# The sum's products of a fused attention and feed-forward kernel come in any order of quads, planned far behind h

## Chip, cores and metric

The kernel runs on one core of a Trainium2 chip. The metric is the device time of one execution in microseconds (us); lower is better. The core's engines are TensorE (PE in the profile; its weight loads are PEld), ScalarE (ACT), VectorE (DVE), GpSimd (POOL) and SyncE (SP), which here only issues DMA transfers. Each engine works through its own instructions in the order of the program.

## What is computed

The input x has 4 batches of 12480 rows with 128 channels. Two attention steps are followed by a feed-forward layer (FFN) over all 49920 rows:

```python
def mab(q, kv):
    s = scale * (q @ kv.transpose(0, 2, 1))
    s = s - s.max(-1, keepdims=True)
    a = np.exp(s)
    a /= a.sum(-1, keepdims=True) + 1e-09
    return a @ kv
h = mab(I, x)                       # 32 inducing rows attend to all x of a batch
attn = mab(x, h)                    # every row attends to the 32 rows of h
...
h = np.maximum(x @ w_in, 0.0)       # x is attn here; w_in is 128 x 2048
return (h * h @ w_out)              # w_out is 2048 x 128
```

All is in fp32. The second attention's weighted sum is not made by itself: since attn is a matrix of weights times the batch's 32 rows, the kernel multiplies those rows by w_in once for each batch (hw in the code) and uses the 32 weights of a row as the FFN's input.

## The kernel before

Rows are taken in **units** of 960, 13 for each batch, 52 in all. For each unit three streams of work are woven together:

- the **first attention** of a unit of the next batch (class First): scores of the 32 inducing rows (sp or na on TensorE, line 430), a running maximum (mx, neg), exponentials (e on ScalarE), transposes (ep, et), a matmul with x (hp or nb, line 484) and the running sums hacc and zs;
- the **second attention** of the unit that comes next (class Second): scores (na, line 626), their eviction ss, transposes (s2t), a softmax in small steps (mx, d, z, rz, d, sk), transposes back (ap, line 687), an eviction sw, and four DMAs on SP that spread sw into st;
- the **FFN** of the present unit (ffn_block), in two blocks of 480 rows. A block goes over the 2048 hidden channels in four **quads** of 512.

Scores of the second attention of unit u+1, of the first attention and its matmul with x are issued together by the function narrow, 32 matmuls, which the text calls a group of small matmuls.

A quad j of a block goes like this. TensorE makes h in two pairs of matmuls, each pair into one of two PSUM buffers (line 782). ScalarE takes the relu of each pair into g (line 790) and then squares the whole of g, 1920 columns, in place (line 801). For fp32 accuracy g is split into hi (rounded to the fp32r type) and lo = g - hi. For even quads VectorE makes hi (line 808); for odd ones a casting DMA of the POOL queue does (line 806, "CAST" in the planner). VectorE makes lo of every quad (line 812). TensorE then makes 12 products (line 825) that add to the block's output sum op in PSUM: four with hi and the high part of w_out (wo_hi), four with hi and its low part (wo_lo), four with lo and wo_hi. After the last quad VectorE transposes op into rows (line 840), and SP stores them.

Buffers: g has four, hi three, lo two, h two, op two.

The order on every engine is set by a **planner** (class Plan) when the program is built. Each step is added as a task with an engine, a cost in ns, a due time, the tasks that it needs and the buffers that it takes or reads. The planner then runs the tasks in an imitated time: of the tasks of an engine that can start within 40 ns of when the engine is free, it takes the one with the earliest due time; otherwise the one that can start first. The costs in its lines (438 for a pair of products, 864 for a relu, 1706 for a square, 2070 for lo) are the author's numbers. Block due times advance by PERIOD / 2 = 16000 ns, quads by part = 4000 ns.

Two rules matter here. First, the six tasks of two products each that make up a quad's 12 are chained: each needs the one before it (last), through all four quads of a block, so the sum goes strictly from quad 0 to quad 3 and through hi with wo_hi, hi with wo_lo and lo in that order. Their due time is the quad's plus 8000 ns, that of the pairs of h two quads later. Secondly, narrow for unit u+1 needs begun, the first matmul of h of unit u.

Of the kernel before, what the change touches and what calls it, by code (L numbers as in the profile page):

```python
# [44 lines left out]
class Plan:  # L45
# [15 lines left out]
    def add(self, engine, ns, fn, due, needs=(), port=False, mode=None, takes=(), reads=(), late=None):  # L61

        if late is None:
            late = self.LATE["PE" if engine == "PE" else "other"] if due > self.begin else 0.0
        needs = [n for n in needs if n is not None]
        t = Task(engine.split("|"), ns, fn, due, needs, port, mode, takes, late, len(self.tasks))  # L70
        for b in list(takes) + list(reads):
            b.users.append(t)
        self.tasks.append(t)
        return t
# [80 lines left out]
def induced_attention_then_squared_relu_ffn(  # L155
# [12 lines left out]
    NF = F // P  # L168
# [4 lines left out]
    NQ = NF // 4  # L173
# [5 lines left out]
    LATE_G1, LATE_OT = 150.0, 400.0  # L179
# [51 lines left out]
    add = plan.add  # L231
# [494 lines left out]
    def narrow(second, f, g, due, step, begun=None):  # L726

        v = {}
        bank_a = Buffer("m") if second or f else None
        bank_b = Buffer("m") if g else None  # L730
        needs = [begun]
        if second:
            needs += [second.s["joined"]]
        if f:
            needs += f.turned
        if g:
            needs += [g.et_done]

        def go():
            if bank_a:  # L740
                v["a"] = bank(f"na_{second.n if second else f.n}")
            if second:
                second.score(v["a"][:, :2 * TS])
            if f:
                f.score(v["a"][:, 2 * TS:4 * TS])
            if g:
                v["b"] = bank(f"nb_{g.n}")
                g.mix(v["b"][:, :C])

        t = add("PE", 510 * bool(second) + 520 * bool(f) + 450 * bool(g), go, due, needs, mode="n",  # L750
                takes=[b for b in (bank_a, bank_b) if b],
                reads=([second.bt] if second else []) + ([f.bt] if f else []) + ([g.bx] if g else []))
        if f:
            f.weigh(t, lambda: v["a"][:, 2 * TS:4 * TS], bank_a, due)
        if second:
            second.weigh(t, lambda: v["a"][:, :2 * TS], bank_a, due, step)
        if g:
            g.add_up(t, lambda: v["b"][:, :C], bank_b, due)


    def ffn_block(b, u, k, second, t0, first_needs):
# [2 lines left out]
        w = {}  # L764
        bo = Buffer("o")
        part = PERIOD / 2 / NQ
        last = None

        def quad(j, last):
            v = {}  # L770
            due = t0 + j * part
            bg, bhi, blo = Buffer("g"), Buffer("hi"), Buffer("lo")
# [44 lines left out]
            for m, (wo, name, from_, buf) in enumerate((  # L817
                (wo_hi, "hi", th, bhi), (wo_lo, "hi", th, bhi), (wo_hi, "lo", tl, blo),
            )):
                for i in range(2):  # L820
                    def products(i=i, wo=wo, name=name, m=m):
                        if j == m == i == 0:
                            w["op"] = ps_o.tile([P, 512], F32, tag="o", name=f"op_{n}")
                        for l in (2 * i, 2 * i + 1):
                            nc.tensor.matmul(  # L825
                                w["op"][:, :BLK], wo[:, 4 * j + l, :], v[name][:, l, :],
                                start=(j == m == l == 0), stop=(j == NQ - 1 and m == 2 and l == 3),
                            )

                    begin = j == m == i == 0  # L830
                    last = add("PE", 438, products, due + 8000 + 600 * (2 * m + i), [from_, last, w_outs[j]],
                               takes=[bo] if begin else [], reads=[buf] + ([] if begin else [bo]))
            return last

        for j in range(NQ):
            last = quad(j, last)

        def rows():
            w["rows"] = att.tile([P, BLK // M, M], F32, tag="rows", name=f"rows_{n}")
# [5 lines left out]

        br = Buffer("rows")
        end = t0 + PERIOD / 2 + 8000
        t = add("DVE", 570, rows, end + 1500, [last], reads=[bo], late=LATE_OT, takes=[br])
        add("SP", 2000, store, end + 4000, [t], reads=[br])
        return w["begun"]  # L850

# [18 lines left out]
    for w, (b, u) in enumerate(units):  # L870
        t_u = t_main + w * PERIOD
        begun = [ffn_block(b, u, k, seconds[w], t_u + k * PERIOD / 2, [opened] if w == 0 else []) for k in range(2)][0]
        nxt = units[w + 1] if w + 1 < len(units) else None
        a = w + NU + 1
        f = g = None
        if a < len(units):
            f = firsts[a] = First(*units[a], t_u + NARROW)
        if a - 1 < len(units):
            g = firsts[a - 1]
        if nxt is None:  # L880
            break
        seconds[w + 1] = Second(*nxt) if nxt[1] else None
        if nxt[1] == 0:
            mix_alone(g, t_u - 2000)
            first_end(nxt[0], t_u, 2000)
            seconds[w + 1] = Second(*nxt)
            narrow(seconds[w + 1], f, None, t_u + NARROW, 1700, begun)
        else:
            narrow(seconds[w + 1], f, g, t_u + NARROW, STEP, begun)
    for t in plan.run():  # L890
        t.fn()

# [30 lines left out]
```

## Time and profile before

| what | us |
|---|---|
| time, median of 3 runs (1910.66 to 1913.94) | 1913.87 |
| the profiled execution's own time | 1910.1 |
| its span, from the first instruction to the last | 1908.3 |
| first and last matmul of h, start | 77.7, 1890.9 |
| mean granted clock of TensorE (1 is full) | 0.986 |

The page gives for each engine its busy time, its share of the span and its number of instructions. A group row gives line, engine, operation, what is written and read, the count, then the busy time in us and the mean of one instruction in ns, then the idle time of the engine ahead of them and what ended most of it. A row of waits reads: engine, tile and line, what it waited for, us in total, times, longest. A timeline row reads: start, length, engine, line, operation, names, count, and in brackets the idle time ahead of it with what ended it. "SPq" is the time in which SP issues a DMA. The end of a matmul is modelled, and a matmul's length includes its way through the array, so that the start of the next one is often earlier than the end shown.

### The profile page before, as it was taken

To read this page: it belongs to the slowest core of one execution; us is meant where nothing else is said; L and a number is where in the kernel's file an instruction comes from. 1 tells how busy PE (TensorE), PEld (TensorE's weight loads), DVE (VectorE), ACT (ScalarE), POOL (GpSimd) and SP (SyncE) were. 2 spreads that over 40 slices of the span, in tenths; PEclk is the share of its full clock that TensorE was granted. 3 is DMA by queue.
4 is the path that set the end of the run, shared out by engine and by line. 5 is a ranking of instruction groups with operands and counts; after the bars stand their busy time and mean duration, and the time that the engine had idled before them with its cause. 6 is when DMAs were issued, how large, how long until landed. Compare 5 with 4: busy or idle time off the path is not lost.

```text
span 1908.3 us, 24030 instructions
## 1 busy us (share of the span) xinstructions
PE 1710.5 (90%) x8897; PEld 1342.1 (70%) x8897; DVE 1462.8 (77%) x1548; ACT 1590.1 (83%) x1602; POOL 128.9 (7%) x230
## 2 busy tenths in 40 slices
PE   7698989889998998989998989899999999998997
PEld 4377767777777777777777767777777777776776
DVE  6677777777887777878787778777777877777776
ACT  5578888788888888888888888888888888888886
POOL 1200000000000000000000000000000000000000
PEclk9799999999999999999999999999999999999999
DMA  9656756666666757667747657667444544444453
GB/s 216 121 156 159 179 159 164 174 159 165 168 165 165 177 163 179 162 173 167 190 141 171 157 170 184 163 164 178 145 140 130 161 148 153 134 152 147 141 159 120
DMA packets 458736, 306.12 MB, mean 160 GB/s; under 512 B 366172, under 2 KB 431484, under 8 KB 458620
## 3 DMA queue, kind: packets, MB, share of 16 engines
q1 hardware_dynamic: 428668, 100.11, 30.7%
q0 software_dynamic: 29952, 204.49, 29.6%
q8 instruction: 70, 1.15, 0.3%
q14 instruction: 46, 0.38, 0.1%
HBM read 48.94 MB, written 25.56 MB: 39 GB/s over the span
## 4 chain that ended last, share of the span: by engine, by line
PE 37%; ACT 21%; issue 15%; DVE 14%; DMA 11%; SPq 2%; DVEq 0%; ACTq 0%; POOLq 0%; POOL 0%
PE op L825 27%; ACT g L790 12%; DVE lo L812 7%; ACT g L801 7%; PE h L782 7%; DMA hi<-g 6%; DVE hi L808 3%; DMA xq<-in_x_dram 3%; SPq L397 1%; DMA words_i<-in_moe_w_in_dram 1%; DVE xt L401 1%; PE wp L586 1%; PE na L626 1%; DVE d L655 1%; ACT d L658 1%
## 5 line engine op out<-in xcount | busy, mean ns | idle before, releaser
L790 ACT ACTIVATE g<-h 128x960 f32<-128x960 f32 x832 | 769.5, 970 | 178.1 <-PE h L782 171.3
L812 DVE TENSOR_TENSOR lo<-g,hi 128x1920 fp32r<-128x1920 f32 x416 | 882.4, 2153 | 36.9 <-DMA hi<-g 28.8
L801 ACT ACTIVATE g<-g 128x1920 f32<-128x1920 f32 x416 | 752.7, 1809 | 5.7
L782 PE MATMUL h<-st,hw 128*128 128x480 f32 x1664 | 481.7, 393 | 104.3 <-ACT g L790 100.0
L825 PE MATMUL op<-hi,wo_hi 128*128 128x480 f32 x1664 | 452.4, 392 | 27.4 <-DMA hi<-g 25.3
L825 PE MATMUL op<-lo,wo_hi 128*128 128x480 f32 x1664 | 429.5, 385 | 17.9 <-DVE lo L812 17.5
L782 PEld LDWEIGHTS h<-st,hw 128*128 128x128 f32 x1664 | 298.4, 189 | 201.1 <-ACT g L790 159.0
L825 PE MATMUL op<-hi,wo_lo 128*128 128x480 f32 x1664 | 429.6, 383 | 0.0
L808 DVE CAST hi<-g 128x1920 fp32r<-128x1920 f32 x208 | 240.8, 1158 | 227.5 <-ACT g L801 226.1
L825 PEld LDWEIGHTS op<-hi,wo_hi 128*128 128x128 f32 x1664 | 303.6, 190 | 103.4 <-DMA hi<-g 41.7
L825 PEld LDWEIGHTS op<-lo,wo_hi 128*128 128x128 f32 x1664 | 305.7, 188 | 81.9 <-DVE lo L812 37.3
L825 PEld LDWEIGHTS op<-hi,wo_lo 128*128 128x128 f32 x1664 | 315.9, 190 | 51.6 <-issue 1.4
L806 POOL DMA_DIRECT2D hi<-g x208 | 110.6, 532 | 1701.6 <-ACT g L801 1366.3
L840 DVE STREAM_TRANSPOSE rows<-op 128x480 f32<-128x480 f32 x104 | 70.7, 679 | 82.6 <-PE op L825 82.6
L658 ACT ACTIVATE d<-d 120x256 f32<-120x256 f32 x52 | 21.7, 417 | 55.4 <-DVE d L655 55.4
L687 PEld LDWEIGHTS ap<-identr,sk 120*128 120x128 f32 x208 | 28.3, 190 | 37.5 <-DVE sk L680 30.6
L687 PE MATMUL ap<-identr,sk 120*128 120x120 f32 x208 | 32.6, 279 | 21.5 <-DVE sk L680 21.2
L401 DVE STREAM_TRANSPOSE xt<-xq 128x960 f32<-128x960 f32 x39 | 45.8, 1174 | 3.9 <-PE na L626 3.8
L651 DVE TENSOR_REDUCE mx<-s2t 120x8 f32<-120x256 f32 x52 | 21.8, 419 | 20.2 <-PE s2t L644 20.0
L662 DVE TENSOR_REDUCE z<-d 120x8 f32<-120x256 f32 x52 | 20.8, 401 | 17.0 <-ACT d L658 17.0
L235 ACT COPY et<-ep 120x256 f32<-120x256 f32 x52 | 19.4, 374 | 16.7 <-PE ep L464 16.0
L626 PE MATMUL na<-xt,hT 128*32 128x240 f32 x416 | 32.7, 387 | 0.0
(91 smaller groups left out, 611.1 us busy)
## 6 DMA issues: line engine op xcount, KB each, us to landing
hi<-g POOLq DMA_DIRECT2D x208, 960.0 KB, 4.1
xn<-in_x_dram SPq DMA_DIRECT2D x52, 480.0 KB, 5.2
st<-sw SPq DMA_DIRECT2D x208, 120.0 KB, 2.3
out_dram<-rows SPq DMA_DIRECT2D x416, 60.0 KB, 2.0
xq<-in_x_dram SPq DMA_DIRECT2D x156, 120.0 KB, 4.4
words_i<-in_moe_w_in_dram SPq DMA_DIRECT2D x4, 512.0 KB, 9.2
words_o<-in_moe_w_out_dram SPq DMA_DIRECT2D x4, 512.0 KB, 7.5
ind_sb<-in_inducing_dram SPq DMA_DIRECT2D x1, 16.0 KB, 1.7
```

Source lines behind the costliest of these rows:

```text
L401: nc.vector.transpose(self.xt, v["xq"].rearrange("p g c -> p (g c)"))
L626: nc.tensor.matmul(where[q * M:(q + 1) * M, :].rearrange("m (k t) -> m k t", k=2), self.s["hT"][:, :M], self.s["xt"][self.u].rearrange("c ...
L658: nc.scalar.activation(v["d"], v["d"], AF.Exp, scale=scale)
L687: nc.tensor.matmul(ap[:, q * TS:(q + 1) * TS], v["sk"][:, q].rearrange("t k a m -> t (k a m)"), identr[:TS, :TS], start=(q == 0), stop=(q ...
L782: nc.tensor.matmul(c["hp"][:, l, :BLK], s["hw"][:, f * P:(f + 1) * P], s["st", u][:, k, :], start=True, stop=True,)
L790: nc.scalar.activation(v["g"][:, 2 * i:2 * i + 2, :], c["hp"][:, :, :BLK], AF.Relu)
L801: nc.scalar.activation(v["g"], v["g"], AF.Square)
L806: nc.gpsimd.dma_start(v["hi"], v["g"])
L808: nc.vector.tensor_copy(v["hi"], v["g"])
L812: nc.vector.tensor_sub(v["lo"], v["g"], v["hi"])
L825: nc.tensor.matmul(w["op"][:, :BLK], wo[:, 4 * j + l, :], v[name][:, l, :], start=(j == m == l == 0), stop=(j == NQ - 1 and m == 2 and l = ...
L840: nc.vector.transpose(w["rows"].rearrange("p g c -> p (g c)"), w["op"][:, :BLK])
```

## The change

The six product tasks of a quad no longer need each other. They need only the first product task of the block, which opens the sum (it takes the PSUM buffer op); which matmul starts and which ends the accumulation is now counted while the program is written out (done). Their due time is the quad's plus 18000 ns in place of 8000. The transpose of op needs all of the block's 24 product tasks (sums) in place of the last. And narrow is called without begun, so it needs only what it reads. The number and shape of TensorE's instructions are unchanged, as are all costs in the planner. Lines behind line 767 have other numbers: h is line 783, the products are 827, lo is 813.

```diff
-        last = None
-
-        def quad(j, last):
+        sums, done = [], []
+
+        def quad(j):
...
-                    def products(i=i, wo=wo, name=name, m=m):
-                        if j == m == i == 0:
+                    def products(i=i, wo=wo, name=name):
+                        if not done:
                             w["op"] = ps_o.tile([P, 512], F32, tag="o", name=f"op_{n}")
                         for l in (2 * i, 2 * i + 1):
+                            done.append(l)
                             nc.tensor.matmul(
                                 w["op"][:, :BLK], wo[:, 4 * j + l, :], v[name][:, l, :],
-                                start=(j == m == l == 0), stop=(j == NQ - 1 and m == 2 and l == 3),
+                                start=len(done) == 1, stop=len(done) == 3 * NF,
                             )
 
-                    begin = j == m == i == 0
-                    last = add("PE", 438, products, due + 8000 + 600 * (2 * m + i), [from_, last, w_outs[j]],
-                               takes=[bo] if begin else [], reads=[buf] + ([] if begin else [bo]))
-            return last
+                    begin = not sums
+                    sums.append(add(
+                        "PE", 438, products, due + 18000 + 600 * (2 * m + i), [from_, w_outs[j]] + sums[:1],
+                        takes=[bo] if begin else [], reads=[buf] + ([] if begin else [bo]),
+                    ))
...
-        t = add("DVE", 570, rows, end + 1500, [last], reads=[bo], late=LATE_OT, takes=[br])
+        t = add("DVE", 570, rows, end + 1500, sums, reads=[bo], late=LATE_OT, takes=[br])
...
-            narrow(seconds[w + 1], f, None, t_u + NARROW, 1700, begun)
+            narrow(seconds[w + 1], f, None, t_u + NARROW, 1700)
         else:
-            narrow(seconds[w + 1], f, g, t_u + NARROW, STEP, begun)
+            narrow(seconds[w + 1], f, g, t_u + NARROW, STEP)
```

What this does to the order is shown at three places. In the names, h_2_6_1_4 is the fifth pair of h (from 0) of batch 2, unit 6, block 1; hi_2_6_0_3 is hi of quad 3 of block 0; the last number of a name only numbers the buffers.

On TensorE, in block 1 of unit 6 of batch 2, before:

```order
L782 MATMUL h_2_6_1_4_10761<-st_2_6_10417,hw_2_8476 128x480 x2
L825 MATMUL op_2_6_1_10766<-hi_2_6_1_0_10758,wo_hi_110 128x480 x4
L825 MATMUL op_2_6_0_10635<-hi_2_6_0_3_10734,wo_hi_110 128x480 x4
L825 MATMUL op_2_6_0_10635<-hi_2_6_0_3_10734,wo_lo_111 128x480 x4
L825 MATMUL op_2_6_1_10766<-hi_2_6_1_0_10758,wo_lo_111 128x480 x4
L782 MATMUL h_2_6_1_5_10790<-st_2_6_10417,hw_2_8476 128x480 x2
L825 MATMUL op_2_6_1_10766<-lo_2_6_1_0_10764,wo_hi_110 128x480 x2
L825 MATMUL op_2_6_0_10635<-lo_2_6_0_3_10780,wo_hi_110 128x480 x4
L825 MATMUL op_2_6_1_10766<-lo_2_6_1_0_10764,wo_hi_110 128x480 x2
L782 MATMUL h_2_6_1_6_10803<-st_2_6_10417,hw_2_8476 128x480 x2
L782 MATMUL h_2_6_1_7_10808<-st_2_6_10417,hw_2_8476 128x480 x2
L782 MATMUL h_2_7_0_0_10820<-st_2_7_10715,hw_2_8476 128x480 x2
```

The same place after the change:

```order
L783 MATMUL h_2_6_1_4_10755<-st_2_6_10447,hw_2_8485 128x480 x2
L827 MATMUL op_2_6_0_10657<-hi_2_6_0_2_10668,wo_lo_111 128x480 x2
L827 MATMUL op_2_6_0_10657<-lo_2_6_0_2_10731,wo_hi_110 128x480 x2
L783 MATMUL h_2_6_1_5_10766<-st_2_6_10447,hw_2_8485 128x480 x2
L827 MATMUL op_2_6_0_10657<-lo_2_6_0_2_10731,wo_hi_110 128x480 x2
L783 MATMUL h_2_6_1_6_10772<-st_2_6_10447,hw_2_8485 128x480 x2
L827 MATMUL op_2_6_0_10657<-hi_2_6_0_3_10721,wo_hi_110 128x480 x4
L827 MATMUL op_2_6_0_10657<-hi_2_6_0_3_10721,wo_lo_111 128x480 x4
L827 MATMUL op_2_6_1_10789<-hi_2_6_1_0_10752,wo_hi_110 128x480 x2
L783 MATMUL h_2_6_1_7_10792<-st_2_6_10447,hw_2_8485 128x480 x2
```

Before, 16 products stand ahead of pair 5 and then three pairs follow each other; now blocks of 4, 2 and 10 products stand between the pairs, and the products belong to quads further back (quad 2 of block 0 behind pair 4 of block 1, where it was quad 0 of block 1).

On TensorE at the start of the main part, before:

```order
L687 MATMUL ap_0_0_945<-identr_94,sk_0_0_938 128x120 x4
L782 MATMUL h_0_0_0_0_968<-st_0_0_955,hw_0_880 128x480 x2
L782 MATMUL h_0_0_0_1_971<-st_0_0_955,hw_0_880 128x480 x2
L626 MATMUL na_0_1_974<-xt_0_1_153,hT_0_878 32x240 x4
L430 MATMUL na_0_1_974<-xt_1_1_900,indT_107 32x240 x4
```

The same place after the change:

```order
L626 MATMUL na_0_1_942<-xt_0_1_153,hT_0_878 32x240 x4
L430 MATMUL na_0_1_942<-xt_1_1_900,indT_107 32x240 x4
L484 MATMUL nb_1_0_951<-xn_1_0_678,et_1_0_872 32x128 x8
L687 MATMUL ap_0_0_993<-identr_94,sk_0_0_938 128x120 x4
L644 MATMUL s2t_0_1_998<-ident_89,ss_0_1_980 120x128 x2
L464 MATMUL ep_1_1_1013<-ident_89,e1_1_1_983 120x128 x2
L626 MATMUL na_0_2_1021<-xt_0_2_183,hT_0_878 32x240 x4
L430 MATMUL na_0_2_1021<-xt_1_2_966,indT_107 32x240 x4
L484 MATMUL nb_1_1_1030<-xn_1_1_759,et_1_1_1018 32x128 x8
L783 MATMUL h_0_0_0_0_1056<-st_0_0_1008,hw_0_880 128x480 x2
```

The groups of small matmuls of units 1 and 2 (na_0_1, na_0_2) now stand ahead of the first pair of h of unit 0.

On SP, the queue that issues the loads and st, at the same place before:

```order
L340 DMA words_o3_876<-in_moe_w_out_dram 128x4x256
L397 DMA xq_1_2_908<-in_x_dram 32x30x32 x4
L702 DMA st_0_0_955<-sw_0_0_951 64x480 x4
L380 DMA xn_1_3_999<-in_x_dram 120x8x128
L397 DMA xq_1_3_1020<-in_x_dram 32x30x32 x4
```

And after the change:

```order
L340 DMA words_o3_876<-in_moe_w_out_dram 128x4x256
L397 DMA xq_1_2_908<-in_x_dram 32x30x32 x4
L380 DMA xn_1_3_964<-in_x_dram 120x8x128
L397 DMA xq_1_3_973<-in_x_dram 32x30x32 x4
L702 DMA st_0_0_1008<-sw_0_0_1002 64x480 x4
```

The loads of a later unit have moved ahead of the spread of st for unit 0, which the first h reads. sw_0_0 itself is now evicted by VectorE, eleven steps behind the last write of sk_0_0; before, ScalarE did it.

More of the change, by code (lines that the diff above doesn't have):

```diff
@@ L820, in quad @@
                 for i in range(2):
-                    def products(i=i, wo=wo, name=name, m=m):
-                        if j == m == i == 0:
+                    def products(i=i, wo=wo, name=name):
+                        if not done:
                             w["op"] = ps_o.tile([P, 512], F32, tag="o", name=f"op_{n}")
                         for l in (2 * i, 2 * i + 1):
+                            done.append(l)
                             nc.tensor.matmul(
                                 w["op"][:, :BLK], wo[:, 4 * j + l, :], v[name][:, l, :],
-                                start=(j == m == l == 0), stop=(j == NQ - 1 and m == 2 and l == 3),
+                                start=len(done) == 1, stop=len(done) == 3 * NF,
                             )
-                    begin = j == m == i == 0
-                    last = add("PE", 438, products, due + 8000 + 600 * (2 * m + i), [from_, last, w_outs[j]],
-                               takes=[bo] if begin else [], reads=[buf] + ([] if begin else [bo]))
-            return last
+                    begin = not sums
[3 more added lines that the diff above has]
+                    ))
         for j in range(NQ):
-            last = quad(j, last)
+            quad(j)
         def rows():
```

## Prediction

> **What bounds the kernel now.** I began with the first part of the page, then took the stretch between the first and the last matmul of h, which holds all 52 units.
>
> ```profile
> PE 1710.5 (90%) x8897; PEld 1342.1 (70%) x8897; DVE 1462.8 (77%) x1548; ACT 1590.1 (83%) x1602; POOL 128.9 (7%) x230
> ```
>
> The windows view of that stretch (busy time of each engine, with its count; granted clock near the end):
>
> ```profile
> 77.70:1890.90 1813.20, 1649.64 (x8380) 1306.88 (x8381) 1403.30 (x1414) 1547.42 (x1499) 112.72 (x212) 0.99 0.60 160
> ```
>
> No engine is full. ScalarE (ACT) works 1547.4 of 1813.2 us and idles 265.8. TensorE's 1649.6 looks fuller than it is, because matmuls overlap. The timeline gives their true pitch and one typical stall; first TensorE, then ScalarE in the same stretch:
>
> ```profile
> 1026.76 0.70 PE L782 MATMUL h<-st,hw 128*128 128x480 f32 x2 [0.64 <-ACT g L790]
> 1027.30 1.91 PE L825 MATMUL op<-hi,wo_hi 128*128 128x480 f32 x8
> 1029.05 1.92 PE L825 MATMUL op<-hi,wo_lo 128*128 128x480 f32 x8
> 1030.81 0.59 PE L782 MATMUL h<-st,hw 128*128 128x480 f32 x2
> ...
> 1025.73 2.74 ACT L790 ACTIVATE g<-h 128x960 f32<-128x960 f32 x3
> 1028.37 1.80 ACT L801 ACTIVATE g<-g 128x1920 f32<-128x1920 f32 x1
> 1031.44 0.97 ACT L790 ACTIVATE g<-h 128x960 f32<-128x960 f32 x1 [1.27 <-PE h L782]
> ```
>
> Eight products start at 1027.30 and the next eight at 1029.05: 1.75 / 8 = 0.219 us each. Sixteen of them, 3.51 us, stand between two pairs of h, and ScalarE, out of h after one square, idles 1.27 us. TensorE had itself waited 0.64 us for ScalarE before that block: the two take turns waiting.
>
> TensorE's own need: each unit has 128 matmuls of 0.219 (28.0 us) and the attention's small ones. Their pitch:
>
> ```profile
> 614.62 0.61 PE L626 MATMUL na<-xt,hT 128*32 128x240 f32 x8
> 615.04 0.59 PE L430 MATMUL na<-xt,indT 128*32 128x240 f32 x8
> 615.45 0.66 PE L484 MATMUL nb<-xn,et 120*32 120x128 f32 x16
> 616.03 1.14 PE L825 MATMUL op<-hi,wo_hi 128*128 128x480 f32 x4
> ...
> 622.71 0.38 PE L644 MATMUL s2t<-ident,ss 128*120 128x128 f32 x2
> 622.84 0.68 PE L782 MATMUL h<-st,hw 128*128 128x480 f32 x2
> ...
> 631.12 0.66 PE L687 MATMUL ap<-identr,sk 120*128 120x120 f32 x4 [0.51 <-DVE sk L680]
> 631.62 0.66 PE L825 MATMUL op<-hi,wo_hi 128*128 128x480 f32 x2
> ```
>
> That is 1.41 + 0.13 (s2t) + as much for ep + 0.50 (ap) = 2.2, so 30.2 us for 39 units; the last 13 have no first attention, 28.0 + 0.42 + 0.13 + 0.50 = 29.1. Sum 39 x 30.2 + 13 x 29.1 = 1556; with some 15 for the h W_in matmuls at three batch ends (an estimate) 1571. So TensorE and ScalarE both need about 1550 to 1570 of 1813 us: neither bounds the stretch alone, their waits do. From the view of waits (total us, times, longest):
>
> ```profile
> DVE hi L808 <- ACT g L801: 226.1, 171, 3.7
> ACT g L790 <- PE h L782: 171.3, 172, 2.9
> ...
> PE h L782 <- ACT g L790: 100.0, 119, 2.2
> DVE rows L840 <- PE op L825: 82.6, 56, 2.7
> ...
> ACT d L658 <- DVE d L655: 55.4, 31, 1.9
> ...
> DVE lo L812 <- DMA hi<-g: 28.8, 28, 3.4
> PE op L825 <- DMA hi<-g: 25.3, 34, 3.4
> ...
> DVE mx L651 <- PE s2t L644: 20.0, 7, 3.6
> ...
> DVE z L662 <- ACT d L658: 17.0, 12, 2.0
> ACT et L235 <- PE ep L464: 16.0, 18, 3.7
> ...
> DVE sw L235 <- PE ap L687: 14.2, 12, 1.6
> ```
>
> ScalarE's 265.8 idle us are 171.3 (h), 55.4 (the softmax's d), 16.0 (et) and 23.1 others. VectorE's wait of 226.1 for squares is what an engine shows that is fed by the slow pair.
>
> **The change part by part.**
>
> *Products behind h.* The matmuls are the same. What moves is h: it comes first whenever its bank is free, and products fill in between. Counted over TensorE's whole order, of 832 pairs of h 174 have 16 or more products ahead of them before the change, and the trace shows 172 waits of ScalarE for h. Afterwards six have more than 12, 72 have 12, 196 have 10. A block of 12 takes 12 x 0.219 = 2.63 us, 0.88 less than the 3.51 after which ScalarE idled 1.27: 0.39 us stays. A block of 10 (2.19 us) leaves 1.27 - 1.32, nothing. So 78 x 0.39 = 31 us of the 171.3 remain. TensorE's need lies 1571 - 1547 = 24 above ScalarE's, which is the same idle time seen from the other side, not a further one. I take 31 and 10 for orders upset by late transfers: 41, with ends of 24 and 171.
>
> What is late next? TensorE's waits for a cast by DMA (25.3) go: between a quad's last h and its first product on a DMA-made hi stand 63 matmuls in the middle, 43 before, so 13.8 us of cover in place of 9.4, against this landing:
>
> ```profile
> hi<-g POOLq DMA_DIRECT2D x208, 960.0 KB, 4.1
> ```
>
> ScalarE's d (55.4): before, it stands behind one square, two relus and small work after the block's first square; now behind two squares and five relus, which at the durations above is 1.80 + 3 x 0.9 = 4.5 us later. VectorE's d itself comes one lo and one transpose (1.18, a row below) later:
>
> ```profile
> L812 DVE TENSOR_TENSOR lo<-g,hi 128x1920 fp32r<-128x1920 f32 x416 | 882.4, 2153 | 36.9 <-DMA hi<-g 28.8
> ```
>
> That is 3.3, so ScalarE gains 1.2 us on waits of 55.4 / 31 = 1.8 us: 0.6 x 31 = 18 stay. et 16 and others 23 stay as they are. New: products lie further behind, so hi (three buffers) and lo (two) are given back later, and VectorE's lo may wait for products. The trace shows no such wait; lo's only wait of note is 28.8 for the cast. Its bounds are 0 and, if every DMA-cast quad waited a microsecond, 208; I take 20, near the row of 28.8, since VectorE has 409.9 idle us in the stretch.
>
> Idle: 41 + 18 + 16 + 23 + 20 = 118. Stretch: 1547.4 + 118 = 1665.
>
> By the Trainium skill, page "Perfetto Trace Analysis", section "Identifying the Most-Contended Engine", matmul busy time says little and the engine of highest occupancy is the contended one, TensorE being judged by weight loading; that makes it ScalarE (83%) with room on TensorE (70%). The row of one kind of them:
>
> ```profile
> L825 PEld LDWEIGHTS op<-lo,wo_hi 128*128 128x128 f32 x1664 | 305.7, 188 | 81.9 <-DVE lo L812 37.3 <-issue 0.6
> ```
>
> The pitch says otherwise: loads of 188 ns every 219 ns are 86% when TensorE is full, so 70% is no room of 30%.
>
> *The second attention without the wait.* In the steady state it moves little: before, the small matmuls (na) of unit u+1 stand one row behind the first h of unit u in nearly every unit; afterwards mostly four to seven rows behind. Only the start and the batch ends put them ahead. At the start two such groups now stand ahead of the first h, and its data comes later. The rows there, on the engine named in each:
>
> ```profile
> 77.68 1.94 PE L782 MATMUL h<-st,hw 128*128 128x480 f32 x4 [3.64 <-DMA st<-sw]
> ...
> 74.66 2.45 SPq L702 DMA_DIRECT2D st<-sw  x4
> ...
> 74.08 0.56 ACT L235 CAST sw<-ap 128x480 fp32r<-128x480 f32 x1 [0.42 <-PE ap L687]
> ...
> 73.69 0.69 DVE L274 SCALAR_TENSOR_TENSOR hc_o<-m_o,hc_o 128x512 f32<-128x512 f32 x1 [0.42 <-ACT m_o L271]
> ...
> 76.13 0.69 DVE L294 SCALAR_TENSOR_TENSOR b_o<-words_o,m_o 128x512 f32<-128x512 uint32 x1
> 80.65 1.18 DVE L401 STREAM_TRANSPOSE xt<-xq 128x960 f32<-128x960 f32 x1 [3.82 <-PE na L626]
> ...
> 82.56 0.29 DVE L500 COPY hacc<-nb 128x128 f32<-128x128 f32 x1
> ```
>
> In the new order sw is made by VectorE, behind the last weight chunk (73.69 to 76.82, 3.1 us) and the five steps from xt to hacc (80.65 to 82.85, 2.2): at 73.69 + 5.3 = 79.0 in place of 74.08. On SP the loads of xn and xq for a later unit now stand ahead of st; xq waits for the transpose in that same chain, so it may add up to 0.9. I take 5.5 us: first h at 83.2; ends 0 and 8. The two groups (about 2 us each on either engine) are then out of the stretch: -4, so it is 1661.
>
> *The end.* Behind the last pair of h stand 50 products now, 36 before: 14 x 0.219 = 3.1 us. But the last square, cast, lo and rows fill that time:
>
> ```profile
> 1890.25 1.03 PE L782 MATMUL h<-st,hw 128*128 128x480 f32 x4
> ...
> 1902.85 0.68 DVE L840 STREAM_TRANSPOSE rows<-op 128x480 f32<-128x480 f32 x1 [1.24 <-PE op L825]
> ```
>
> From 1890.9 to the span's end are 17.4 us; I take 18.4. Products of two blocks interleave on two banks, as they did before: 0.
>
> Sum: 83.2 + 1661 + 18.4 + 1.8 (this execution took 1910.1 us, its span 1908.3) = 1764.4, say 1765. The execution lies 0.2% below the median of 1913.87; I leave that.
>
> **The rivals.**
>
> *Nearly full (chance 0.17).* ScalarE never waits for h beyond TensorE's need (24 for 41), d's wait goes (18) and lo never waits (20): 55 less, about 1710. For it: only six long blocks remain. Against: the order is fixed, while transfers scatter. By the skill's section named above, with ScalarE alone the bound, this is how it would go.
>
> *VectorE becomes the bound (0.22).* Its waits for rows, ScalarE's d, s2t and sw stay (rows and sw alone 96.8; with z 17.0 and mx 20.0, 133.8), and each of the 208 casts holds up lo by 1 us: 1403.3 + 133.8 + 208 = 1745, and 83.2 + 1745 + 20.2 = 1848. For it: lo on a cast quad needs the landing at once, and deferring products gives it no cover. The Trainium skill, page "SBUF — State Buffer", section "Who interferes with whom", says that a VectorE op in a two-port mode locks out GpSimd, which then can't write a DMA's descriptors; a denser VectorE would so delay casts. Against: 28 such waits in 208 so far.
>
> *Slower (0.08).* lo's two buffers: the products that free them run 24 matmuls (5.3 us) later behind their quad's last h than before (77 for 53, in the middle), so lo waits for TensorE, g is not freed, ScalarE stops. With w us for each of 416 lo: 1403.3 + 133.8 + 28.8 + 416 w. It equals 1813 at w = 0.59; at w = 0.7 the stretch is 1857 and the time 1960. Against: the order places lo's products by when the buffers come free, and no lo waits on TensorE's products now.
>
> *It does nothing (0.03).* ScalarE's 171.3 only turn into waits of TensorE at h, because blocks are as long in sum: 1910. Against: the two engines' idle time now alternates, and both are idle at once in none of the rows above.
>
> **How the numbers follow.** Forecast 1765, by itself 1735 to 1805, chance 0.50. With nearly full down to 1690 and VectorE's case up to 1860 the range holds about 0.8; left out are slower, no effect and the far parts. Faster by over 0.2% (some 4 us, about what a measurement of this kernel tells from no change): 0.50 + 0.17 + 0.22 = 0.89; within it 0.03; slower 0.08.
>
> **What would show it.** Right: ScalarE's wait for h (171.3) falls below 60 and its idle time in the stretch from 266 to about 120; TensorE's wait for casts goes to near 0; first h at 81 to 85; ScalarE busy above 90% in the middle slices. VectorE's case: lo waits for casts above 150 us. Slower: a row of lo waiting for op above 250. Wrong altogether: the wait for h stays above 120 with blocks of 10 products ahead of it, which would mean that the block's length was not its cause.

## The result and the profile after

The changed kernel takes 1687.28 us (median of 4 runs, 1685.28 to 1689.03), the kernel before beside it 1913.90. The ratio is 0.8817, with a 95% interval of 0.8799 to 0.8834: 11.8% less time. The forecast of 1765 had the direction right and was 78 us too high; the result lies 2.7 us below the range.

The first part of the page of the changed kernel, busy time and share of each engine:

```profile
PE 1639.3 (97%) x8897; PEld 1352.1 (80%) x8897; DVE 1451.2 (86%) x1544; ACT 1573.1 (93%) x1606; POOL 129.1 (8%) x230
```

The stretch between its first and last matmul of h, by the windows view:

```profile
84.80:1666.20 1581.40, 1570.44 (x8301) 1311.21 (x8298) 1384.00 (x1394) 1529.08 (x1499) 111.68 (x210) 1.00 0.69 182
```

And its chain that ended last, by engine (before, TensorE held 37% of it):

```profile
PE 89%; DMA 4%; ACT 3%; DVE 2%; issue 1%; SPq 0%; POOL 0%; ACTq 0%; DVEq 0%; POOLq 0%
```

The profiled execution took 1685.96 us, 224.1 less than the one before. All of it comes from the stretch, 1581.4 in place of 1813.2 (231.8 less); the first h comes 7.1 us later (84.8 for 77.7) and the tail is 0.6 longer. ScalarE idles 1581.4 - 1529.1 = 52.3 us in the stretch, before 265.8. The waits of the changed kernel (total, times, longest):

```profile
ACT g L791 <- PE h L783: 38.9, 70, 3.5
DVE lo L813 <- PE op L827: 38.1, 51, 2.4
...
DVE lo L813 <- DMA hi<-g: 12.3, 12, 3.4
...
PE op L827 <- DMA hi<-g: 4.1, 5, 2.9
...
PE h L783 <- DMA st<-sw: 3.9, 2, 2.3
...
PE h L783 <- ACT g L791: 3.2, 4, 1.8
```

TensorE's own waits, 100.0 for ScalarE and 25.3 for casts before, are 3.2 and 4.1. Its timeline shows one unit from the small matmuls of one to those of the next:

```profile
1012.73 0.61 PE L626 MATMUL na<-xt,hT 128*32 128x240 f32 x8
...
1043.19 0.61 PE L626 MATMUL na<-xt,hT 128*32 128x240 f32 x8
```

That is 30.46 us, where the prediction had worked out 30.2 as what TensorE needs. In the last batch it is 29.35, for 29.1:

```profile
1320.69 0.61 PE L626 MATMUL na<-xt,hT 128*32 128x240 f32 x8
1350.04 0.61 PE L626 MATMUL na<-xt,hT 128*32 128x240 f32 x8
```

So TensorE looks full. Whether it is the bound, and which part of the change brought it there, the experiments ask. Each kernel below is given as its edit against the changed kernel, unless said otherwise, with its ratio to the kernel before on the same chip and the 95% interval. A point is one per cent of the time before. Part one of the change is the free order and the late due time of the products, part two the missing wait of narrow for begun.

### The profile page after: what moved, and what is told of

The parts are those of the page before. It is cut to its first block, busy times and chain, and to the rows that moved or that the text cites. A ratio compares the mean times of both kernels' runs of the same rounds, so it can differ in the third digit from the quotient of the medians.

```text
span 1684.2 us, 24215 instructions
## 1 busy us (share of the span) xinstructions
PE 1639.3 (97%) x8897; PEld 1352.1 (80%) x8897; DVE 1451.2 (86%) x1544; ACT 1573.1 (93%) x1606; POOL 129.1 (8%) x230
## 4 chain that ended last, share of the span: by engine, by line
PE 89%; DMA 4%; ACT 3%; DVE 2%; issue 1%; SPq 0%; POOL 0%; ACTq 0%; DVEq 0%; POOLq 0%
PE op L827 61%; PE h L783 20%; DMA hi<-g 2%; PE na L626 2%; ACT g L791 2%; ACT g L802 1%; PE ap L687 1%; PE wp L586 1%; PE nb L484 1%; PE na L430 1%; DMA xn<-in_x_dram 1%; PE s2t L644 1%; DMA st<-sw 1%; DMA words_o<-in_moe_w_out_dram 1%; DMA words_i<-in_moe_w_in_dram 1%
## 5 line engine op out<-in xcount | busy, mean ns | idle before, releaser
L813 DVE TENSOR_TENSOR lo<-g,hi 128x1920 fp32r<-128x1920 f32 x416 | 886.8, 2150 | 59.8 <-PE op L827 38.1
L791 ACT ACTIVATE g<-h 128x960 f32<-128x960 f32 x832 | 777.5, 969 | 43.4 <-PE h L783 38.9
L783 PE MATMUL h<-st,hw 128*128 128x480 f32 x1664 | 505.5, 386 | 7.1 <-DMA st<-sw 3.9
L827 PE MATMUL op<-hi,wo_hi 128*128 128x480 f32 x1664 | 471.2, 384 | 4.1 <-DMA hi<-g 4.1
L827 PE MATMUL op<-hi,wo_lo 128*128 128x480 f32 x1664 | 461.3, 382 | 0.0
L827 PE MATMUL op<-lo,wo_hi 128*128 128x480 f32 x1664 | 450.9, 382 | 0.3 <-DVE lo L813 0.3
L783 PEld LDWEIGHTS h<-st,hw 128*128 128x128 f32 x1664 | 301.5, 189 | 75.0 <-ACT g L791 17.1
L827 PEld LDWEIGHTS op<-hi,wo_hi 128*128 128x128 f32 x1664 | 308.5, 188 | 60.9 <-issue 8.8
L827 PEld LDWEIGHTS op<-lo,wo_hi 128*128 128x128 f32 x1664 | 310.7, 188 | 48.8 <-DVE lo L813 0.7
L235 ACT COPY xt<-xtp 128x480 f32<-128x480 f32 x26 | 14.4, 557 | 14.5 <-PE xtp L415 14.4
L464 PE MATMUL ep<-ident,e 128*120 128x128 f32 x104 | 21.2, 286 | 4.6 <-ACT e L456 2.2
L456 ACT ACTIVATE e<-na,neg 128x240 f32<-128x240 f32 x39 | 17.8, 456 | 7.8 <-DVE ss L235 3.6
L651 DVE TENSOR_REDUCE mx<-s2t 120x8 f32<-120x256 f32 x52 | 21.2, 407 | 4.2 <-PE s2t L644 4.0
```

Source lines behind the costliest of these rows:

```text
L464: nc.tensor.transpose(v["ep"][:TS, k * P:(k + 1) * P], v["e"][:, k * TS:(k + 1) * TS], ident)
L783: nc.tensor.matmul(c["hp"][:, l, :BLK], s["hw"][:, f * P:(f + 1) * P], s["st", u][:, k, :], start=True, stop=True,)
L791: nc.scalar.activation(v["g"][:, 2 * i:2 * i + 2, :], c["hp"][:, :, :BLK], AF.Relu)
L813: nc.vector.tensor_sub(v["lo"], v["g"], v["hi"])
L827: nc.tensor.matmul(w["op"][:, :BLK], wo[:, 4 * j + l, :], v[name][:, l, :], start=len(done) == 1, stop=len(done) == 3 * NF,)
```

## The experiments: which engine is the bound

Less work for ScalarE, with the order unchanged:

```diff
-                nc.scalar.activation(v["g"], v["g"], AF.Square)
+                nc.scalar.activation(v["g"][:, :2, :], v["g"][:, :2, :], AF.Square)
```

> The changed kernel with the square over half of g's columns (the other half is left out; all orders are the same): ScalarE has some 0.85 us less in each of 416 quads, about 350 us. If TensorE bounds the changed kernel: 1670 to 1690 us, no more than 1% off, and TensorE's pitch stays at 30.4 us per unit. If ScalarE bounds it or both do by turns: 1560 to 1640.

Measured: 1679.79 us, 0.8789 [0.8774, 0.8804], 0.3 points below the changed kernel. ScalarE's busy time falls from 1573.1 to 1249.1 us, and the time hardly follows:

```profile
PE 1639.7 (98%) x8897; PEld 1361.2 (81%) x8897; DVE 1449.3 (86%) x1544; ACT 1249.1 (74%) x1606; POOL 128.4 (8%) x230
```

Its waits, where the freed time shows as ScalarE's idle time:

```profile
ACT g L791 <- PE h L783: 305.8, 279, 5.3
...
ACT d L658 <- DVE d L655: 30.0, 41, 1.8
...
ACT et L235 <- PE ep L464: 7.4, 8, 1.9
```

And TensorE's pitch in it, 30.37 us:

```profile
1012.09 0.61 PE L626 MATMUL na<-xt,hT 128*32 128x240 f32 x8
1042.46 0.61 PE L626 MATMUL na<-xt,hT 128*32 128x240 f32 x8
```

ScalarE is not the bound. The d and et waits, nearly gone in the changed kernel, are back here and cost nothing; that matters below.

Less work for TensorE, with the planner unchanged:

```diff
-                        for l in (2 * i, 2 * i + 1):
+                        for l in (2 * i, 2 * i + 1) if wo is not wo_lo else ():
...
-                                start=len(done) == 1, stop=len(done) == 3 * NF,
+                                start=len(done) == 1, stop=len(done) == 2 * NF,
```

> The changed kernel without the products with the low part of w_out (4 of 12 per quad are left out; the planner still counts them): TensorE has 1664 x 0.219 = 364 us less. If TensorE alone bounds the changed kernel, the time falls until the next engine is full: ScalarE's 1529 busy us in place of a stretch of 1581, so 1620 to 1660 us. If ScalarE bounds it: within 0.5% of 1687. If VectorE or casts hold it: within 0.5% too, with rising waits of lo.

Measured: 1652.28 us, 0.8644 [0.8629, 0.8660]. TensorE now waits for ScalarE, 353 times:

```profile
PE h L783 <- ACT g L791: 152.6, 353, 2.0
...
ACT g L791 <- PE h L783: 9.8, 6, 3.1
```

So TensorE bounds the changed kernel, and ScalarE stands right behind it: with a quarter of the unit's 128 large matmuls gone, only 2% of the time goes (0.8644 for 0.8817).

The same question to the kernel before, with the edit of the first of the two:

> The kernel before with the square over half of g's columns (the other half is left out): ScalarE has about 350 us less to do. If before no engine was the bound and the two took turns waiting, the time falls by what TensorE waited for ScalarE and little else: 1780 to 1850 us, while ScalarE's wait for h grows above 300. If ScalarE was the bound: below 1700. If the chain of products alone was: 1880 to 1914.

Measured: 1859.48 us, 0.9716 [0.9694, 0.9739]. Taking over 300 us of work from ScalarE gains 52 (1911.73 on the same chip), between the first range expected (1780 to 1850 us) and the third (1880 to 1914). So ScalarE's work did not bound the kernel before either: most of the freed time turns into its idle time at h, which grows to 416 us.

```profile
ACT g L790 <- PE h L782: 416.2, 327, 4.9
...
PE h L782 <- ACT g L790: 63.5, 109, 1.4
```

## The experiments: which part of the change did it

The products late, but still in one chain, and narrow still behind begun. This is the kernel before with one number changed:

```diff
-                    last = add("PE", 438, products, due + 8000 + 600 * (2 * m + i), [from_, last, w_outs[j]],
+                    last = add("PE", 438, products, due + 18000 + 600 * (2 * m + i), [from_, last, w_outs[j]],
```

> The kernel before with the products' due time at the quad's plus 18000 ns, but still chained in the order of the quads, and the second attention waiting as before. Theory A (due time): 8 blocks of 14 or more products are left, so 1690 to 1740 us and ScalarE's wait for h 40 to 70. Theory B (the fixed order): 1840 to 1910, with TensorE's wait for casts at 20 to 60 us as before.

Measured: 1719.25 us, 0.8959 [0.8941, 0.8977], in Theory A's range. Of ScalarE's wait at h, 171.3 us before, 71.1 are left, just above that theory's 70, and ScalarE hardly waits for d and et any more:

```profile
ACT g L790 <- PE h L782: 71.1, 85, 3.8
...
ACT et L235 <- PE ep L464: 2.4, 3, 1.0
ACT d L658 <- DVE d L655: 2.1, 2, 1.8
```

Part one whole, free order and late, with narrow still behind begun:

```diff
-            narrow(seconds[w + 1], f, None, t_u + NARROW, 1700)
+            narrow(seconds[w + 1], f, None, t_u + NARROW, 1700, begun)
...
-            narrow(seconds[w + 1], f, g, t_u + NARROW, STEP)
+            narrow(seconds[w + 1], f, g, t_u + NARROW, STEP, begun)
```

> The changed kernel with the second attention again waiting for the first matmul of h of the unit ahead: the first part of the change alone. Main theory (the order of the sum's products does it, the missing wait nearly nothing): 1675 to 1700 us, with the first matmul of h back near 78 us (84.8 in the changed kernel) and a pitch of 30.4 to 30.8 us per unit in the middle. Rival (the second attention's earlier start feeds h): 1720 to 1800, with waits for st or for the softmax ahead of h. By the count of blocks of 14 or more products ahead of a pair of h (15 here, 6 in the changed kernel, 182 before) ScalarE's wait for h should be 40 to 70 us.

Measured: 1719.29 us, 0.8963 [0.8942, 0.8985]. While narrow waits, the free order adds nothing to the late due time; my 1675 to 1700 for it was a miss, since the missing wait is worth another 1.5 points in the changed kernel. The free order without the late due time, with narrow behind begun by the two lines above:

```diff
-                        "PE", 438, products, due + 18000 + 600 * (2 * m + i), [from_, w_outs[j]] + sums[:1],
+                        "PE", 438, products, due + 8000 + 600 * (2 * m + i), [from_, w_outs[j]] + sums[:1],
```

> The kernel before with the chain of products taken away, but their due time still the quad's plus 8000 ns, and the second attention waiting as before. Theory A (what costs is that products stand ahead of h, so the due time is what matters): 135 blocks of 14 or more products stay (182 before), so 1840 to 1900 us, with ScalarE's wait for h at 110 to 160 us. Theory B (what costs is the fixed order of the sum, which makes TensorE stand behind a late cast): 1690 to 1760, with TensorE's wait for casts near 5 us and ScalarE's wait for h below 60.

Measured: 1949.18 us, 1.0160 [1.0129, 1.0191]: 1.6% slower than before, which neither expectation held. In this order 135 pairs of h have 14 or more products ahead of them (182 before, 6 in the changed kernel). Its waits:

```profile
ACT g L791 <- PE h L783: 245.0, 259, 5.8
...
PE h L783 <- ACT g L791: 110.0, 133, 2.2
```

ScalarE and TensorE take turns as before, and one such turn in its timeline reads as the one in the prediction does; first TensorE, then ScalarE:

```profile
1010.08 0.70 PE L783 MATMUL h<-st,hw 128*128 128x480 f32 x2 [1.12 <-ACT g L791]
1010.77 1.57 PE L827 MATMUL op<-hi,wo_hi 128*128 128x480 f32 x6
1012.19 1.05 PE L827 MATMUL op<-hi,wo_lo 128*128 128x480 f32 x4
1013.07 0.60 PE L827 MATMUL op<-hi,wo_hi 128*128 128x480 f32 x2
1013.51 1.04 PE L827 MATMUL op<-hi,wo_lo 128*128 128x480 f32 x4
1014.39 0.59 PE L783 MATMUL h<-st,hw 128*128 128x480 f32 x2
...
1015.02 0.97 ACT L791 ACTIVATE g<-h 128x960 f32<-128x960 f32 x1 [1.52 <-PE h L783]
```

Sixteen products stand ahead of a pair of h and ScalarE idles 1.52 us. So it is the late due time that breaks up the blocks (8 of 14 or more are left with it alone); order freed without it does not. Why it is slower than the kernel before, with fewer long blocks, stays open. TensorE's waits for casts are 45.8 us (25.3 before), and its granted clock is a little lower, 0.972 to 0.979 for 0.983 to 0.987 of the kernel before beside it.

The fourth corner, the chain kept with the late due time and without the wait for begun:

```diff
-                    last = add("PE", 438, products, due + 8000 + 600 * (2 * m + i), [from_, last, w_outs[j]],
+                    last = add("PE", 438, products, due + 18000 + 600 * (2 * m + i), [from_, last, w_outs[j]],
...
-            narrow(seconds[w + 1], f, None, t_u + NARROW, 1700, begun)
+            narrow(seconds[w + 1], f, None, t_u + NARROW, 1700)
...
-            narrow(seconds[w + 1], f, g, t_u + NARROW, STEP, begun)
+            narrow(seconds[w + 1], f, g, t_u + NARROW, STEP)
```

(against the kernel before)

> The changed kernel with the old chain through the six product tasks kept; due time (+18000) and the missing wait as in the changed kernel. With the run that has the chain, the late due time and the wait (0.8959) and the one without chain that has the wait (0.8963) this fills the table of two by two. Theory (distance): what part two gains is set by where the last matmul of a unit's second attention (ap) lands ahead of the unit's first h. Of 52 units 38 have fewer than 40 matmuls between them here; the changed kernel has 12 (0.8817), the runs with 32 to 44 stood at 0.896 to 0.907. So 0.894 to 0.907 of the time before, 1711 to 1736 us, with TensorE waiting 15 us or more at h for st. Rival: the missing wait is itself the gain, whatever the order: 0.880 to 0.887, 1684 to 1698 us, TensorE's wait for st below 8 us.

Measured: 1742.51 us, 0.9090 [0.9070, 0.9110], a little above the theory's end and far from the rival's. So the missing wait gains 1.5 points where the order is free and loses 1.3 where it is chained: by itself it is no gain. Seen the other way, the free order is worth 2.7 points without the wait and nothing with it. The late due time alone makes 10.4 of the 11.8 points. The missing wait in the kernel before, with nothing else changed, was not tried.

## The experiments: the second attention's way to the first h

What the missing wait changes is where the planner puts the second attention. I counted TensorE's matmuls from the first of the four that end a unit's second attention (ap) to the unit's first h, the four included; expectations that say 13 for the changed kernel count one unit more than the 12 in the table below. Between the two lie an eviction to sw, four DMAs on SP and their landing. How long that can take is seen in the kernel with the chain, late and without the wait, where h came late for it:

```profile
681.98 0.56 PE L687 MATMUL ap<-identr,sk 120*128 120x120 f32 x4
...
684.25 0.65 ACT L235 CAST sw<-ap 128x480 fp32r<-128x480 f32 x1
...
684.92 4.25 SPq L702 DMA_DIRECT2D st<-sw  x4
...
690.49 0.68 PE L782 MATMUL h<-st,hw 128*128 128x480 f32 x2 [1.36 <-DMA st<-sw]
```

From ap to h are 8.51 us, as much as 39 matmuls of 0.219. This is one unit: over the 52 of this kernel, the time from the first ap to the landing of the last st lies between 5.4 and 11.8 us, with a median of 8.3. So a unit with fewer than about 40 matmuls on this way can make TensorE wait, and need not; here 38 units have fewer, and TensorE waits for st 21 times. The late due time itself shortens the way, since it takes products away from ahead of h: its median is 68 matmuls before the change, 34 with part one alone and 54 in the changed kernel. Two more kernels vary this with no change to part one: the wait put back for the first three units alone,

```diff
-            narrow(seconds[w + 1], f, g, t_u + NARROW, STEP)
+            narrow(seconds[w + 1], f, g, t_u + NARROW, STEP, begun if w < 3 else None)
```

> The changed kernel with the wait for begun put back for the first three units alone; the other 48 units do not wait. The order that the planner then finds is close to that with the wait everywhere: 47 of 52 units have fewer than 40 matmuls between ap and the first h. Theory (distance): as with the wait everywhere, 0.893 to 0.900, 1709 to 1722 us, TensorE's wait at h for st 15 us or more. Rival (the missing wait itself): 49 of 52 units have none here, so 0.880 to 0.886, 1684 to 1696 us.

and the wait gone everywhere, with narrow's due time 1000 ns earlier:

```diff
-    PERIOD, START, T_MAIN, NARROW, STEP = 32000.0, 2600.0, 66000.0, 6000.0, 1700.0
+    PERIOD, START, T_MAIN, NARROW, STEP = 32000.0, 2600.0, 66000.0, 5000.0, 1700.0
```

> The changed kernel with the second attention's due time 1000 ns earlier and nothing else. In the order 8 blocks of 14 or more products are left, but in 34 units fewer than 40 matmuls stand between the second attention's last matmul and the first h (13 in the changed kernel, 47 or so in the kernel with the first part alone). If that distance decides: 1705 to 1730 us, with TensorE's wait for st at 15 to 30 us. If the missing wait itself was what helped: 1683 to 1692.

Three more give the products other due times, the wait gone everywhere: +28000, +40000 and +13000 ns in place of +18000.

> The changed kernel with the products' due time at the quad's plus 28000 ns. In the order 7 blocks of 14 or more products stand ahead of h (6), and in 4 units fewer than 40 matmuls stand between the second attention's last matmul on TensorE and the unit's first h (13 in the changed kernel). If these two counts decide: 1680 to 1692 us. If the size of the deferral itself does, as 13000 and 40000 suggest at first sight: 1692 to 1700, between 18000 and 40000.

> The changed kernel with the products' due time at the quad's plus 40000 ns: so far behind that the buffers alone bring products forward. 32 blocks of 14 or more products stand ahead of pairs of h (6 in the changed kernel). If h first is all that matters: 1685 to 1710 us. If products too far behind hold hi and lo and stop VectorE: above 1720, with lo and hi waiting for products above 150 us (38 and 12 in the changed kernel).

> The changed kernel with the products' due time at the quad's plus 13000 ns in place of 18000: the size of the deferral. 6 blocks of 14 or more products and 88 of 12 stand ahead of pairs of h (6 and 72 in the changed kernel). If it only matters that h comes first: 1680 to 1700 us. If the backlog of products itself carries TensorE over late casts, less of it costs: 1710 to 1760 with TensorE's wait for casts above 20 us.

Measured, in the order of the ratio:

| kernel | units with under 40 matmuls from ap to h | TensorE's wait at h for st, us (times) | time, us | ratio |
|---|---|---|---|---|
| the changed kernel | 12 of 52 | 3.9 (2) | 1687.28 | 0.8817 [0.8799, 0.8834] |
| +28000 | 4 | 5.7 (2) | 1696.57 | 0.8850 [0.8824, 0.8876] |
| +40000 | 4 | 5.0 (4) | 1699.99 | 0.8890 [0.8871, 0.8909] |
| wait for the first three units | 47 | 19.5 (14) | 1706.71 | 0.8919 [0.8884, 0.8954] |
| chain, late, wait kept | 32 | 16.1 (9) | 1719.25 | 0.8959 [0.8941, 0.8977] |
| free, late, wait kept | 44 | 21.2 (13) | 1719.29 | 0.8963 [0.8942, 0.8985] |
| narrow 1000 ns earlier | 34 | 32.1 (22) | 1729.76 | 0.9024 [0.8999, 0.9049] |
| +13000 | 36 | 29.6 (22) | 1741.69 | 0.9071 [0.9045, 0.9096] |
| chain, late, no wait | 38 | 32.6 (21) | 1742.51 | 0.9090 [0.9070, 0.9110] |

The three kernels with few short ways are the three fastest, and the six with many are slower, whether they wait for begun or not; the kernel that waits for begun in three units alone loses most of what the missing wait brings. Among the kernels with many short ways the count does not rank them, the wait for st does roughly. All nine have a later due time than the kernel before. That kernel and the one with the free order alone have few short ways too, 9 and 4, and are slower than all nine, so the way counts only once the blocks are broken up.

Not every expectation held. The three-unit kernel came out at 1706.71 us, between its two ranges: its loss is smaller than with the wait everywhere. The kernel with narrow 1000 ns earlier fell into the range of the distance, with a wait for st just above its 30 us. The +28000 kernel came out at 1696.57 us, in the range of the size of the deferral and not in that of the two counts, so the counts do not decide alone. The +40000 kernel, with 32 blocks of 14 or more, stayed in the range of "h first". The +13000 kernel came out in the second of its two ranges, but not by the reason given there: TensorE's waits for casts are 8.5 us, for the 20 or more expected.

Does the late st itself cost this, or does it only go with it? In the next kernel st is loaded from a constant tile, so that it needs nothing of the second attention; free, late, wait kept, the same order:

```diff
-                            v["sw"][k * 64:(k + 1) * 64, :].bitcast(F32),
+                            w_in_sb[k * 64:(k + 1) * 64, :BLK],
```

> The kernel with the first part alone (order and deferral changed, the second attention waiting as before), in which st is loaded from a tile that never changes (w_in) in place of sw: h no longer waits for the unit's second attention, and the output leaves the second attention's weights out. All orders are the same. Theory (the second attention's data come too late for h: 21 us of TensorE's waits for st in 13 units): 1690 to 1702 us, that is 17 to 29 us less than 1719, with no wait for st. Rival (the order itself is worse, its blocks and gaps differ: 15 blocks of 14 or more products for 6): 1712 to 1722, with ScalarE's wait for h still above 60.

Measured: 1701.31 us, 0.8878 [0.8848, 0.8907], in the theory's range. TensorE still waits three times for the constant st:

```profile
PE h L783 <- DMA st<-w_in_sb: 3.6, 3, 1.4
```

Of the 1.46 points between 0.8963 and 0.8817 the constant st takes away 0.85, some 16 of 28 us. I put these down to the late st and the other 0.6 points to the order itself; the changed kernel with a constant st, which would test this split, was not run. The same constant st in the +13000 kernel:

> The changed kernel with the due time of the products at 13000 ns, and st loaded from the unchanging tile as well (the second attention's weights are left out). All orders are those of the run with 13000. Theory (its 54 us over the changed kernel come from st too: 29.6 us of waits in 22 units): 1705 to 1718 us. Rival (the shorter backlog leaves TensorE without products while ScalarE and VectorE are busy with the attention): 1730 to 1745.

Measured: 1768.00 us, 0.9214 [0.9181, 0.9247], slower than with the late st and outside both ranges expected. There the theory fell. Its waits show what came in its place:

```profile
ACT g L791 <- PE h L783: 115.7, 113, 5.3
PE op L827 <- DMA hi<-g: 58.4, 46, 3.4
DVE lo L813 <- DMA hi<-g: 37.6, 36, 3.5
```

My reading, which no further run tests: at +13000 products stand so close behind their quad's square that without the pauses for st they reach TensorE before the cast has landed (58.4 us, 8.5 with the late st), and ScalarE's h waits behind them (115.7 us, 66.9 with the late st). The granted clock is a little lower too, 0.973 to 0.980 for 0.984 to 0.988. What +13000 costs in all is so not settled. It also shows that a constant st does more than take a wait away, so the 0.85 points above are the sum of all that it does there.

## Why the prediction was too high

**The cause was right.** Blocks of products ahead of h made ScalarE and TensorE wait in turns; the late due time alone takes the ratio from 1 to 0.896, and the free order that keeps long blocks gives nothing. TensorE's waits for casts went, as forecast.

**The 41 us left at h were right by luck.** Of ScalarE's 171.3 us at h the forecast left 41, and 38.9 are left, but not where it put them. It had 0.39 us at each of 78 blocks of 12 or more (30 us; the prediction says 31) and nothing at blocks of 10. Matched with the order, 48 of the 70 waits, 25.6 us, stand at blocks of 10; the 72 blocks of 12 have 2.8 us and longer ones 5.7. Nor was the wait before all of this kind: blocks of 14 or more held 118 of the 171.3 us, and 39 waits with 38.7 us stood behind fewer than ten products and a group of small matmuls or a transpose.

**The step that failed** is the sum: it built the stretch on ScalarE's 1547.4 busy us and added idle time that was held to stay, "et 16 and others 23 stay as they are", d's 18, and the 20 for lo, where the stretch had become TensorE's. The groups of ScalarE in the stretch (busy, mean ns, idle time before them) show what was left:

```profile
L791 ACT ACTIVATE g<-h 128x960 f32<-128x960 f32 x831 | 776.5, 969 | 43.4 <-PE h L783 38.9 <-DVE lo L813 2.3 <-DVE mx L443 1.0
L802 ACT ACTIVATE g<-g 128x1920 f32<-128x1920 f32 x414 | 749.9, 1811 | 6.9
...
L658 ACT ACTIVATE d<-d 120x256 f32<-120x256 f32 x50 | 20.7, 414 | 0.0
...
L235 ACT COPY et<-ep 120x256 f32<-120x256 f32 x37 | 13.6, 368 | 0.1
```

Idle time of 118 became 52.3: 65.7 us of the miss. Term by term, d's 18 and et's 16 became 0.0 and 0.1, the 20 for lo 2.3, and the others' 23 some 11. VectorE's lo does wait for products, 38.1 us for the 20 forecast, but ScalarE feels 2.3 of it. Waits for d and et look like those of an engine that runs ahead of its inputs. With the late due time alone they are 2.1 and 2.4 us; with half the squares left out, 30.0 and 7.4, in a kernel that is no slower. They could not be added to the work of an engine that has no time to run ahead.

**ScalarE's 1547.4 was no floor.** As many instructions in the stretch, 1499, are busy 1529.1 us, though the relu still takes 969 ns and the square 1811. Its timeline in the changed kernel:

```profile
1014.80 1.81 ACT L802 ACTIVATE g<-g 128x1920 f32<-128x1920 f32 x1
1016.51 1.81 ACT L791 ACTIVATE g<-h 128x960 f32<-128x960 f32 x2
```

The square of 1.81 us is followed after 1.71: what comes right behind overlaps its end by 0.10, and each wait that goes gives back such an overlap. Added up one by one, the 1499 durations are 1656.3 us before and 1655.1 after; 1048 pairs of neighbours overlapped by 108.9 us in all before, and 1184 by 126.0 after, which is 17.1 of the 18.3 us; the other 1.2 are in the durations. The Trainium skill, page "ScalarE: Activation LUTs", section "What ACT_TABLE_LOAD costs", gives an overlap of about 93 ns for activations back to back; the trace, with 0.10 us, agrees. The 65.7 and 18.3 are 84.0, and less the 4 taken off for the start they are the stretch's miss of 79.6 (1661 for 1581.4).

**The bound stood in the text.** TensorE's need was put at 1571, and the stretch came out 10 above it. With 83.2 + 1571 + 18.4 + 1.8 = 1674 the bound was 12 below the profiled execution; the sum of waits, 1661 for the stretch, lay 90 above it. The rival "nearly full", 1710, came nearest and still kept et and the others. The Trainium skill, page "Perfetto Trace Analysis", section "Identifying the Most-Contended Engine", has TensorE's room judged by its weight loads, which before the change were busy 70%. Here the measurement decides against 30% of room: full, TensorE shows PEld at 80%.

**Part two was mis-sized.** "In the steady state it moves little" was wrong: in the changed kernel it is worth 1.5 points, for more than half of which the late st stands above. That the way from ap to h had a price at all was not in the sum, nor that part one would shorten it. The start's number was about right: first h at 84.8 for 83.2. But with free, late products and the wait kept it came at 80.8, so the missing wait costs 4.0 of the 5.5 forecast, and some 3 come with part one, which the forecast had at nothing. The path was another, too, as the timeline of the changed kernel shows: sw waited for ap and not for VectorE's steps, and before ap TensorE idled 4.91 us:

```profile
79.49 1.11 PE L687 MATMUL ap<-identr,sk 120*128 120x120 f32 x4 [4.91 <-ACT e L456]
80.64 0.66 DVE L235 CAST sw<-ap 128x480 fp32r<-128x480 f32 x1 [0.71 <-PE ap L687]
81.32 2.43 SPq L702 DMA_DIRECT2D st<-sw  x4
...
84.85 1.84 PE L783 MATMUL h<-st,hw 128*128 128x480 f32 x4
```

**The other rivals fell.** VectorE as the bound asked for lo's waits for casts above 150 us: they are 12.3, and casts land as before:

```profile
hi<-g POOLq DMA_DIRECT2D x208, 960.0 KB, 4.2
```

The Trainium skill, page "SBUF — State Buffer", section "Who interferes with whom", describes a lock-out of GpSimd by VectorE. No run here shows it: with VectorE's share up from 77% to 86% the median landing of a cast went from 4.1 to 4.2 us. Lo's two buffers asked for waits for op above 250: they are 38.1.

**What stays open.** The 0.6 points by which the free, late order with the wait is slower than the changed kernel even with a constant st; the price of +13000; and why the free order alone is slower than the kernel before.

## What to carry to other kernels

Where two nearly full engines wait for each other in turns, work out what each needs back to back and forecast from the larger need, not from the busy time plus the waits that seem untouched: waits of an engine that runs ahead can vanish when it no longer does, as d's and et's did here. On an in-order engine that feeds a full one, put the feeding work first and let the work that nobody waits for fall far behind; here a due time did that, and freeing the order without it made the kernel 1.6% slower. How far behind matters too: of the due times tried, +28000 and +40000 were 0.3 and 0.7 points slower than +18000, and +13000 2.5. And when such an order comes out of a planner, count in it the distance behind every transfer that the next stage needs, since a small change elsewhere can move it below the time that the transfer takes.

## What the hardware showed unexpectedly

ScalarE's busy time in a profile depends on how often it waits: 1547.4 against 1529.1 us for 1499 instructions whose durations add up to 1656.3 and 1655.1, as the overlap of 0.10 us between one instruction and the next is lost at each wait. And a TensorE that is the bound, with waits of some 11 us for ScalarE, casts and st together, shows weight loads busy for 80% of the span and not more.
